# Decode attention in four layers: the last output-projection rows over six DMA engines, a bridge of matmuls, a split wo block and a mended head mapping

## Chip, cores, metric

One core of one Trainium2 chip runs the whole program. The metric is device time in microseconds (us); less is better. Each kernel was run several times; all runs quoted here are of the fast state. The profile is one execution, and its times count from the start of its span.

## The reference

Four layers, A, B, A, B, each a residual step of one token. A and B have their own caches and weights; each has 32 heads of width 192, 8192 cached positions and a model width of 640, in bfloat16.

```python
h = layernorm(x)                               # [1, 640]
q = (h @ wq).reshape(32, 192)                  # wq [640, 6144]
p = softmax(q @ k_cache^T * 192**-0.5)         # k_cache [32, 8192, 192]
o = p @ v_cache                                # v_cache [32, 8192, 192]
x = x + o.reshape(6144) @ wo                   # wo [6144, 640]
```

One K or V head is 3 MB. Of the 256 that the four layers use, 250 are loaded from memory (the page counts the loads), so the program is a stream of loads with arithmetic beside it.

## The kernel before

SyncE issues all loads into a pool of 8 slots. VectorE multiplies K by the query, TensorE sums the products, and TensorE multiplies V by the probabilities. The output projection takes 30 heads in three blocks of 10 (`wo`, 1920 rows on 128 partitions). The last two heads come apart, as `wol`: 384 rows of wo, 480 KB, 3 rows for each of 128 partitions. In the last layer, 3 of the 15 row groups of the third block come as a load of their own, `wob`, after `wol`.

```python
# the load of the last rows: one transfer over 128 partitions
if O_PART[l] == P:
    return SP.op(lambda s: s.dma_start(
        wol_rows(l), w["wo"][r0:r0 + O_LAST * DH].rearrange("(p i) n -> p (i n)", p=P)),
        *free, sem=semOL, inc=16)
...
# order of the last steps of a layer: V of heads 28 to 31, the block wo 2, then wol
part += [("v", l, i) for i in range(H - AHEAD, H)]
part.insert(-O_LAST, ("wc", l, 2))
part.insert(-1 if l == 1 else len(part), ("wo", l, 2))   # in layer 1 before V of head 31
...
# a head's gather is kept in `todo` and done at a later step
elif n[0] == "wo":
    if todo is not None:
        todo(); todo = None
    ...
else:                                                     # wol: does not do what is in todo
    last["TT"] = last["TTn"]
    last["oTl"] = ev_y = project(n, wol_rows(l), oTl[0:O_PART[l]], last["TTn"])
```

Two faults stand in it. In layer 1 the V of head 31 is the last step before `wol`, and `wol` does not do the gather that waits in `todo`, so that layer projects an old output of head 31. In layer 3, where heads are taken in another order, `q_spread` and `gather` use the position of a head where they need its number.

Of the kernel before, what the change touches and what calls it, by code (L numbers as in the profile page):

```python
# [71 lines left out]
def build(nc, A_x, A_k, A_v, A_wq, A_wo, B_x, B_k, B_v, B_wq, B_wo, out):  # L72
# [12 lines left out]
    TS = J * DH  # L85
    QW = H * DH
    Q_PARTS = [[(0, 2), (2, 2), (4, 1)] if l < 2 else [(0, 1), (1, 2), (3, 2)] for l in range(NL)]
    O_PART = [P] * NL
    OI = [O_LAST * DH // n for n in O_PART]
    NB = 3  # L90
    G = 4
    FORWARD = dict(heads=list(range(H)), q0=0, q1=Q_FIRST * DH, wo=[0, HEADS_W, 2 * HEADS_W], wol=H - O_LAST)
    BACKWARD = dict(heads=[H - 2, H - 1] + list(range(H - HEADS_W, H - 2)) + list(range(O_LAST, H - HEADS_W))
# [4 lines left out]
    with ExitStack() as ctx:  # L98
# [12 lines left out]
        wq0 = [sb(f"wq0{i}", [P, DC, Q_FIRST * DH], BF16) for i in range(2)]  # L111
        orow = sb("orow", [1, HEADS_W * DH], BF16)
        oT = sb("oT", [P, NW], BF16)
        oTl = sb("oTl", [P, max(OI)], BF16)
        o_sb = sb("o_sb", [P, 2 * DH], F32)
        q_sb = [sb(f"q_sb{i}", [P, DH], BF16) for i in range(3)]
        qT = sb("qT", [P, H * DH // P], BF16)
# [65 lines left out]
        def head(l, p):  # L183
            return ORDER[l]["heads"][p]
# [12 lines left out]
        for l in range(NL):  # L197
            if l < 2:
                plan.append(("wq", l, 0))
                steps += [("wq", l, g) for g in range(3)]  # L200
            elif l == 2:
                plan += [("wq", l, g) for g in range(3)]
                steps.append(("wq", l, 0))
            else:
                plan.append(("wq", l, 0))
                steps.append(("wq", l, 0))
            for p in range(H):
                if p in (HEADS_W, 2 * HEADS_W):
                    b = p // HEADS_W - 1
                    steps += [("wc", l, b), ("wo", l, b)]  # L210
                    plan.append(("wo", l, b))
                if first_load("k", l, p) == ("k", l, p):
                    plan.append(("k", l, p))
                if stays("k", l, p):
                    plan.append(("t", l, p))
                if l == 2 and p == 0:
                    part = [("m", l, 0), ("wq", l, 1), ("s", l, 0), ("v", l, 0), ("wq", l, 2)]
                elif p < H - AHEAD:
                    part = [("m", l, p), ("s", l, p), ("v", l, p)]
                else:  # L220
                    part = [("m", l, p)]
                    if p > H - AHEAD:
                        part.append(("s", l, p - 1))
                    if p == H - 1:
                        part.append(("s", l, p))
                        part += [("v", l, i) for i in range(H - AHEAD, H)]
                        part.insert(-O_LAST, ("wc", l, 2))
                        part.insert(-1 if l == 1 else len(part), ("wo", l, 2))
                steps += part
                plan += [n for n in part if n[0] == "wo" or n[0] == "v" and first_load(*n) == n]  # L230
                if l == 3 and p == 1:
                    for g in (1, 2):
                        plan.append(("wq", l, g))
                        steps.append(("wq", l, g))
            plan.append(("wol", l))
            steps.append(("wol", l))
        plan.append(("wob", NL - 1))
        at = {n: i for i, n in enumerate(steps)}

        def released(n):  # L240
# [40 lines left out]
                return pool[:, i + c0 * QW:i + (c0 + k) * QW].rearrange("p (c n) -> p c n", c=k)  # L281
            return slot[place[("wq", l, g)]][:, 0:k * QC].rearrange("p (c n) -> p c n", c=k)

        def wol_rows(l):

            if l + 1 == NL:
                i = place[("wol", l)] * TS
            else:
                i = place[("wq", l + 1, 0)] * TS + (DC * QW if l == 0 else QC)
            return pool[0:O_PART[l], i:i + OI[l] * D]  # L290

        def transfer(n):
            l = n[1]
# [2 lines left out]
            free = [freed[b] for b in before[n]]  # L296
            if n[0] == "wol":
                r0 = o["wol"] * DH
                if O_PART[l] == P:
                    return SP.op(lambda s: s.dma_start(  # L300
                        wol_rows(l), w["wo"][r0:r0 + O_LAST * DH].rearrange("(p i) n -> p (i n)", p=P)),
                        *free, sem=semOL, inc=16)
                k = O_PART[l] // O_LAST
                for h in range(O_LAST):
                    e = SP.op(lambda s, h=h: s.dma_start(
                        wol_rows(l)[h * k:(h + 1) * k],
                        w["wo"][r0 + h * DH:r0 + (h + 1) * DH].rearrange("(q e i) n -> e q (i n)", e=8, i=OI[l])),
                        *free, sem=semOL, inc=16)
                return e
            if n[0] == "t":  # L310
# [68 lines left out]
        def layer(l, ev_z, ev_true):  # L379
# [56 lines left out]

            def q_spread(h):

                c0 = h * DH
                PE.wait(last["qT"], last["QB"], ev_const)  # L440
                done = 0
                while done < DH:
                    b, o = divmod(c0 + done, P)
                    n = min(P - o, DH - done)
                    e = PE.op(lambda t, b=b, o=o, n=n, d=done: t.matmul(  # L445
                        QM[:, d:d + n], lhsT=qT[:, b:b + 1].broadcast_to([P, P]), rhs=ident[:, o:o + n],
                        start=True, stop=True), signal=(done + n == DH), bank=use["QM"])
                    done += n
                last["qbc"] = e
                i = (l * H + h) % 3  # L450
                ev_q[h] = last["QB"] = AC.op(
                    lambda a: a.activation(q_sb[i][:], QM[:, 0:DH], ACT.Copy), e, last["q"][i], bank=use["QM"])  # L452
# [2 lines left out]

            def project(n, rows, o, ev_o):

                t3 = rows.rearrange("p (i n) -> p i n", n=D)
                k = t3.shape[1]
                end = n == ("wob", l) or n == ("wol", l) and l + 1 < NL  # L460
                PE.wait(ev_o, need(n), last["YB"])
                for i in range(k):
                    for c in range(DC):
                        e = PE.op(lambda t, i=i, c=c, f=y_first[0], fin=end and i == k - 1: t.matmul(  # L464
                            YB[:, c:c + 1], lhsT=t3[:, i, c:D:DC], rhs=o[:, i:i + 1], start=f, stop=fin,
                            skip_group_check=True), signal=(i == k - 1 and c == DC - 1), bank=use["YB"])
                        y_first[0] = False
                freed[n] = e
                return e

            def columns(k):

# [62 lines left out]
            def values(h):  # L535
# [16 lines left out]
                if h < H - O_LAST:  # L552
                    parts = [(o_sb[:], OB[par][:, 0:2 * DH])]
                else:
                    q = 1 if O_PART[l] == P else O_PART[l] // O_LAST // 8
                    parts = [(o_sb[:, i * DH:(i + 1) * DH].rearrange("p (i e q) -> p q e i", i=OI[l], q=q),
                              OB[par][:, i * DH:(i + 1) * DH].rearrange("p (q e i) -> p q e i", i=OI[l], q=q))
                             for i in range(2)]
                for o, i in parts:
                    ev_os[h] = AC.op(lambda a, o=o, i=i: a.activation(o, i, ACT.Copy, scale=rl[pi][:, 0:1]),  # L560
                                     e, ev_rl[h], last["osb"], bank=use[f"O{par}"])
                last["O"][par] = last["rl"][pi] = ev_os[h]

            def gather(h):

                PE.wait(ev_os[h], last["TO"], ev_const)
                for i in range(2):
                    e = PE.op(lambda t, i=i: t.matmul(TB[0:1, C_O:C_O + DH], lhsT=pick[:, i:i + 1],  # L568
                                                      rhs=o_sb[:, i * DH:(i + 1) * DH], start=(i == 0), stop=(i == 1)),
                              signal=(i == 1), bank=use["TB"])  # L570
                last["osb"] = e
                o0 = (h % HEADS_W) * DH
                last["TO"] = last["row_written"] = AC.op(
                    lambda a: a.activation(orow[0:1, o0:o0 + DH], TB[0:1, C_O:C_O + DH], ACT.Copy), e, last["orow"], bank=use["TB"])  # L574

            def gather_last(h):

                n = O_PART[l] // O_LAST
                k = OI[l]
                r0 = (h - (H - O_LAST)) * n  # L580
                PE.wait(ev_os[h], last["TT"], ev_const)
                for c in range(k):
                    for i in range(2):
# [11 lines left out]
            for i, n in enumerate(here):  # L595
# [20 lines left out]
                elif n[0] == "wo":  # L616
# [1 line left out]
                        todo()  # L618
                        todo = None
                    k = NW - NB if n == ("wo", NL - 1, 2) else NW  # L620
                    last["oT"] = project(n, slot[place[n]][:, 0:k * D], oT[:, 0:k], last["oTw"])
                else:
                    last["TT"] = last["TTn"]
                    last["oTl"] = ev_y = project(n, wol_rows(l), oTl[0:O_PART[l]], last["TTn"])
                    if l + 1 == NL:
                        ev_y = project(("wob", l), slot[place[("wo", l, 2)]][:, (NW - NB) * D:NW * D], oT[:, NW - NB:NW], last["oTw"])
                following = [m[2] for m in here[i + 1:] if m[0] == "m" and m[2] not in ev_q][:1]
                if q_ready and following and n[0] in ("m", "v", "wc", "wo", "wq") and (n[0] == "wq" or following[0] <= n[2] + 2):
                    q_spread(following[0])
# [66 lines left out]
```

## Time and profile before

| | before |
|---|---|
| time, median (3 runs) | 1997.03 us (1996.98 to 1997.15) |
| moved | 849.67 MB, mean 426 GB/s |
| busy: TensorE, VectorE | 70%, 53% of the span |

The first lines are from the profile's page: the span, then the span in 40 equal slices, with DMA busy in tenths and GB/s.

```profile
span 1994.7 us, 20387 instructions
...
DMA  9999999999999999999999999999999999999998
GB/s 411 431 431 428 431 428 430 430 432 429 429 429 431 428 432 429 429 431 428 430 384 431 430 429 432 428 430 429 430 430 426 429 431 429 431 429 430 430 429 344
DMA packets 40487, 849.67 MB, mean 426 GB/s; under 512 B 4688, under 2 KB 4688, under 8 KB 5328
```

The stream runs at about 430 GB/s everywhere but at the start, in the slice of the passage from layer 1 to layer 2 (384) and at the end (344).

The passage between layers 1 and 2, from the timeline (start, duration, engine, line, operation, output<-inputs, shapes, count; in brackets the idle time before and what ended it):

```profile
1010.47 3.16 PE L464 MATMUL YB<-oT,pool 128*128 128x1 bf16 x75
...
1017.58 2.73 PE L545 MATMUL O<-pool,p_sb 128*2 128x384 bf16 x32 [3.96 <-DMA pool<-in_B_v_cache_dram]
...
1020.24 0.77 PE L464 MATMUL YB<-oTl,pool 128*128 128x1 bf16 x15
1020.36 0.95 ACT L560 ACTIVATE o_sb<-O,small 128x192 f32<-128x192 f32 x2 [9.62 <-PE O L545]
...
1034.77 0.34 SPq L321 DMA_DIRECT2D pool<-in_A_k_cache_dram  x1
```

TensorE waits 3.96 us for V of head 31, multiplies it, and projects the last rows at 1020.24, before head 31's output has been evicted (1020.36): the missing gather can be seen. The K load of layer 2 is issued only at 1034.77: by the view of waits, SyncE's queue waits 8.7 us for the score matmuls of layer 2 (L58) that free its slot, and these come after the projection. The groups of instructions show the missing gather by number: 84 matmuls are 7 heads of 12, where four layers have 8 such heads:

```profile
L584 PE MATMUL TB<-small,o_sb 128*64 128x1 f32 x84 | 6.0, 199 | 7.3 <-ACT o_sb L560 7.3
```

The tail of the last layer, from the same view. The last load, `wob`, lands at 1989.98; the last matmul ends 1.5 us later:

```profile
1987.69 2.56 PE L464 MATMUL YB<-oT,pool 128*128 128x1 bf16 x60 [1.17 <-DMA pool<-in_B_wo_dram]
...
1990.11 0.74 PE L464 MATMUL YB<-oTl,pool 128*128 128x1 bf16 x15
...
1990.71 0.74 PE L464 MATMUL YB<-oT,pool 128*128 128x1 bf16 x15
```

One more thing is in the trace, but in no view: the times at which each of the 16 engines reports the landing of its share of a load. They show how far engines have drifted apart. The table was made from these records: the last landing of a load, and how far ahead of it the other engines were.

```
before, last wo block, layer 0: last 510.44, the others ahead by 4.8 4.7 4.6 4.5 4.4 4.4 | 3.1 2.5 | 1.6 ... 1.3 us
before, last wob:               last 1989.98, the others ahead by 8.2 8.2 8.0 8.0 7.4 7.1 | 5.7 4.0 | 2.0 ... 0.5 us
```

Six engines run far ahead. They gain nothing by it, for a wait ends with the last of the 16 reports: for V of head 31 of layer 1 the first comes at 1009.67 us, the last at 1017.53, and TensorE starts on it at 1017.58.

### The profile page before, as it was taken

The numbers are of one execution on the slowest core, as the hardware profiler recorded it, in microseconds if no ns is written. First come the engines' busy times: TensorE is split into PE (matmuls) and PEld (weight loads), VectorE is DVE, ScalarE is ACT, GpSimd is POOL, SyncE is SP. The second block draws the span as 40 slices with busy tenths as digits, with TensorE's granted clock in tenths as the row PEclk, the third lists the DMA queues.
The fourth block names the chain that finished last, engine by engine and source line by source line (L and its number), as shares of the span: only waits on it lengthen the run. The fifth ranks groups of instructions, "written<-read, shape, count | busy, mean of one in ns | idle before, by whom it ended". The sixth has DMA issues, their size and how long they took to land.

```text
span 1994.7 us, 20387 instructions
## 1 busy us (share of the span) xinstructions
PE 1392.3 (70%) x10426; PEld 317.9 (16%) x7482; DVE 1047.4 (53%) x1074; ACT 220.2 (11%) x664; POOL 4.5 (0%) x22
## 2 busy tenths in 40 slices
PE   4766767667567766766767676676776777766776
PEld 1111112111311111211031111111112212111112
DVE  3554554556255455455726545545563466554563
ACT  0111111110011111111011111111101111111111
POOL 0000000000000000000000000000000000000000
PEclk9888887888688788888978888878887878888888
DMA  9999999999999999999999999999999999999998
GB/s 411 431 431 428 431 428 430 430 432 429 429 429 431 428 432 429 429 431 428 430 384 431 430 429 432 428 430 429 430 430 426 429 431 429 431 429 430 430 429 344
DMA packets 40487, 849.67 MB, mean 426 GB/s; under 512 B 4688, under 2 KB 4688, under 8 KB 5328
## 3 DMA queue, kind: packets, MB, share of 16 engines
q1 hardware_dynamic: 40256, 848.38, 99.4%
q8 instruction: 70, 1.15, 0.2%
q14 instruction: 17, 0.14, 0.0%
q10 hardware_dynamic: 144, 0.00, 0.0%
HBM read 848.36 MB, written 0.00 MB: 425 GB/s over the span
## 4 chain that ended last, share of the span: by engine, by line
DMA 69%; PE 17%; DVE 12%; ACT 1%; issue 1%; another core or an unknown queue 0%; DVEq 0%
DMA pool<-in_B_k_cache_dram 32%; DMA pool<-in_A_k_cache_dram 30%; PE S L58 11%; DVE pool L494 10%; DMA pool<-in_B_wo_dram 2%; PE O L545 2%; DMA pool<-in_A_wo_dram 2%; DMA pool<-in_B_v_cache_dram 2%; DMA x_bf<-in_A_x_dram 1%; PE S L507 1%; PE TB L568 1%; PE QT L426 1%; DVE s_sb L515 1%; ACT p_sb L525 1%; PE YB L464 1%
## 5 line engine op out<-in xcount | busy, mean ns | idle before, releaser
L494 DVE TENSOR_TENSOR pool<-pool,q_sb 128x3072 bf16<-128x3072 bf16 x512 | 865.5, 1752 | 406.2 <-DMA pool<-in_A_k_cache_dram 207.6
L58 PE MATMUL S<-pool,ident 128*128 128x512 bf16 x2944 | 796.8, 425 | 35.4 <-DVE pool L494 35.4
L545 PE MATMUL O<-pool,p_sb 128*2 128x384 bf16 x4096 | 346.9, 420 | 4.0 <-DMA pool<-in_B_v_cache_dram 4.0
L507 PE MATMUL S<-pool,ident 128*128 128x512 bf16 x128 | 59.7, 467 | 224.7 <-DVE pool L494 224.7
L515 DVE TENSOR_REDUCE s_sb<-S 128x64 f32<-128x512 f32 x128 | 88.3, 690 | 229.2 <-PE S L58 229.2
L568 PE MATMUL TB<-o_sb,small 128*1 128x192 f32 x480 | 123.6, 390 | 38.2 <-DVE small L533 27.1
L545 PEld LDWEIGHTS O<-pool,p_sb 128*2 128x2 bf16 x4096 | 127.9, 88 | 138.0 <-issue 99.2
L452 ACT ACTIVATE q_sb<-QM 128x192 bf16<-128x192 f32 x120 | 39.6, 330 | 956.5 <-PE QM L445 956.5
L445 PEld LDWEIGHTS QM<-ident,qT 128*128 128x128 bf16 x240 | 23.1, 98 | 739.3 <-issue 723.9
L529 PE MATMUL TB<-small,ones 128*128 128x1 f32 x256 | 50.3, 266 | 109.9 <-ACT p_sb L525 109.9
L519 PE MATMUL QM<-ident,m_bf 128*128 128x128 bf16 x128 | 27.8, 217 | 122.9 <-DVE m_bf L518 121.2
L560 ACT ACTIVATE o_sb<-O,small 128x384 f32<-128x384 f32 (+1 forms) x136 | 77.2, 579 | 238.5 <-PE O L545 238.5
L533 DVE RECIPROCAL small<-TB 128x1 f32<-128x1 f32 x128 | 21.5, 168 | 123.0 <-PE TB L529 123.0
L525 ACT ACTIVATE p_sb<-s_sb,small 128x64 bf16<-128x64 f32 x128 | 44.5, 348 | 269.6 <-DVE small L522 269.6
L522 DVE TENSOR_REDUCE small<-QM 128x1 f32<-128x128 f32 x128 | 37.3, 291 | 62.1 <-PE QM L519 62.1
L574 ACT ACTIVATE orow<-TB 1x192 bf16<-1x192 f32 x120 | 38.3, 319 | 202.2 <-PE TB L568 202.2
L529 PEld LDWEIGHTS TB<-small,ones 128*128 128x128 f32 x256 | 39.5, 194 | 130.4 <-ACT p_sb L525 130.4
L507 PEld LDWEIGHTS S<-pool,ident 128*128 128x128 bf16 x128 | 12.7, 99 | 283.9 <-DVE pool L494 283.6
L519 PEld LDWEIGHTS QM<-ident,m_bf 128*128 128x128 bf16 x128 | 12.3, 96 | 215.6 <-ACT q_sb L452 126.9
L568 PEld LDWEIGHTS TB<-o_sb,small 128*1 128x1 f32 x480 | 33.4, 89 | 81.5 <-DVE small L533 36.0
L464 PE MATMUL YB<-oT,pool 128*128 128x1 bf16 x900 | 38.0, 178 | 5.8 <-DMA pool<-in_A_wo_dram 2.3
L464 PEld LDWEIGHTS YB<-oT,pool 128*128 128x128 bf16 x900 | 37.0, 131 | 6.7 <-ACT oT L478 2.9
(50 smaller groups left out, 213.9 us busy)
## 6 DMA issues: line engine op xcount, KB each, us to landing
pool<-in_B_k_cache_dram SPq DMA_DIRECT2D x64, 3072.0 KB, 35.5
pool<-in_A_k_cache_dram SPq DMA_DIRECT2D x63, 3072.0 KB, 27.6
pool<-in_A_v_cache_dram SPq DMA_DIRECT2D x63, 3072.0 KB, 33.7
pool<-in_B_v_cache_dram SPq DMA_DIRECT2D x60, 3072.0 KB, 36.5
pool<-in_A_wo_dram SPq DMA_DIRECT2D x6, 2400.0 KB, 25.5
pool<-in_B_wo_dram SPq DMA_DIRECT2D x5, 2400.0 KB, 34.0
pool<-in_A_wq_dram SPq DMA_DIRECT2D x1, 7680.0 KB, 20.7
pool<-in_B_wq_dram SPq DMA_DIRECT2D x1, 7680.0 KB, 30.5
```

What stands on the lines that cost most here:

```text
L58: return t.add_instruction(mybir.InstMatmult(name=t.bass.get_next_instruction_name(), engine=mybir.EngineType.PE, ins=[t.lower_ap(rhs), t. ...
L452: lambda a: a.activation(q_sb[i][:], QM[:, 0:DH], ACT.Copy), e, last["q"][i], bank=use["QM"])
L464: e = PE.op(lambda t, i=i, c=c, f=y_first[0], fin=end and i == k - 1: t.matmul(YB[:, c:c + 1], lhsT=t3[:, i, c:D:DC], rhs=o[:, i:i + 1], s ...
L494: e = DV.op(lambda v, d0=d0: v.tensor_tensor(k3[:, :, d0:d0 + QD], kin[:, :, d0:d0 + QD], q_sb[qi][:, d0:d0 + QD].unsqueeze(1).broadcast_t ...
L507: t.matmul(S[:, :], lhsT=ident[:], rhs=k3[:, :, d0:d0 + R], start=True, stop=fin) if d0 == 0 else
L515: ev_s = DV.op(lambda v: v.tensor_reduce(s_sb[par][:], S[:].rearrange("p (j r) -> p j r", r=R), AX.X, ALU.add), ev_S[h], last["s"][par], b ...
L519: e = PE.op(lambda t: t.matmul(QM[:, C_MX:C_MX + P], lhsT=m_bf[par][:, 0:1].broadcast_to([P, P]), rhs=ident[:], start=True, stop=True), ev ...
L525: ev_p[h] = AC.op(lambda a: a.activation(p_sb[pi][:], s_sb[par][:], ACT.Exp, bias=negm[par][:, 0:1], accum_out=l_col[par][:]), ev_n, ev_s, ...
L529: e = PE.op(lambda t: t.matmul(TB[:, C_L + par:C_L + par + 1], lhsT=ones[:, 0:1].broadcast_to([P, P]), rhs=l_col[par][:], start=True, stop ...
L545: e = PE.op(lambda e, g=g, j=j, f=m < G, fin=fin: e.matmul(OB[par][32 * g:32 * g + 2, 0:2 * DH], lhsT=p_sb[pi][:, j:j + 2], rhs=t[:, j * D ...
L560: ev_os[h] = AC.op(lambda a, o=o, i=i: a.activation(o, i, ACT.Copy, scale=rl[pi][:, 0:1]), e, ev_rl[h], last["osb"], bank=use[f"O{par}"])
L568: e = PE.op(lambda t, i=i: t.matmul(TB[0:1, C_O:C_O + DH], lhsT=pick[:, i:i + 1], rhs=o_sb[:, i * DH:(i + 1) * DH], start=(i == 0), stop=( ...
```

## The change

Its intent is to give the last rows to engines that are ahead. The author's assumption was that a load split over 6 engines goes to the six that run ahead and relieves the others; the rows move to 48 + 48 partitions (0 to 47 and 64 to 111), 4 rows each, for that. Beside this the change mends the two faults, puts 8 matmuls of no use ("bridging") into layer 1, meant to keep the TensorE clock up while it waits for V (in the profile of before the granted clock is 0.5 from 1011.65 to 1032.13 us, and the 3.96 us of waiting are in it), and in layer 3 splits the last wo block in 8 + 7 row groups, both ahead of `wol`.

```diff
-    O_PART = [P] * NL
-    OI = [O_LAST * DH // n for n in O_PART]
-    NB = 3
+    LE = 6
+    LP = LE * 8
+    OI = DH // LP
+    NB = 7
+    WARM = 8
...
+            if l + 1 == NL:
+                plan.append(("wob", l))
+                steps.append(("wob", l))
             plan.append(("wol", l))
             steps.append(("wol", l))
-        plan.append(("wob", NL - 1))
...
-            return pool[0:O_PART[l], i:i + OI[l] * D]
+            return pool[64 * h:64 * h + LP, i:i + OI * D]
...
                 for h in range(O_LAST):
                     e = SP.op(lambda s, h=h: s.dma_start(
-                        ...
+                        wol_rows(l, h), w["wo"][r0 + h * DH:r0 + (h + 1) * DH].rearrange("(q e i) n -> e q (i n)", e=LE, i=OI)),
                         *free, sem=semOL, inc=16)
...
-                c0 = h * DH
+                c0 = head(l, h) * DH - ORDER[l]["q1"] + Q_FIRST * DH
...
+            def warm():
+                t3 = slot[place[("v", l, H - 2)]]
+                PE.wait(last["S"][1])
+                for i in range(WARM):
+                    PE.op(... SP_[1][:, :], lhsT=ident[:], rhs=t3[:, i * 512:(i + 1) * 512] ...)
...
-                o0 = (h % HEADS_W) * DH
+                o0 = (head(l, h) - ORDER[l]["wo"][h // HEADS_W]) * DH
...
                 else:
+                    if todo is not None:
+                        todo()
+                        todo = None
                     last["TT"] = last["TTn"]
```

(Cut: the projection over two halves of rows, and the permutation of the last heads' outputs that fits the new place of the rows.)

More of the change, by code (lines that the diff above doesn't have):

```diff
@@ L113, in build @@
         oT = sb("oT", [P, NW], BF16)
-        oTl = sb("oTl", [P, max(OI)], BF16)
+        oTl = sb("oTl", [P, OI], BF16)
         o_sb = sb("o_sb", [P, 2 * DH], F32)
@@ L282, in wq_rows, with wol_rows @@
             return slot[place[("wq", l, g)]][:, 0:k * QC].rearrange("p (c n) -> p c n", c=k)
-        def wol_rows(l):
+        def wol_rows(l, h):
             if l + 1 == NL:
@@ L298, in transfer @@
                 r0 = o["wol"] * DH
-                if O_PART[l] == P:
-                    return SP.op(lambda s: s.dma_start(
-                        wol_rows(l), w["wo"][r0:r0 + O_LAST * DH].rearrange("(p i) n -> p (i n)", p=P)),
-                        *free, sem=semOL, inc=16)
-                k = O_PART[l] // O_LAST
                 for h in range(O_LAST):
                     e = SP.op(lambda s, h=h: s.dma_start(
-                        wol_rows(l)[h * k:(h + 1) * k],
-                        w["wo"][r0 + h * DH:r0 + (h + 1) * DH].rearrange("(q e i) n -> e q (i n)", e=8, i=OI[l])),
+                        wol_rows(l, h), w["wo"][r0 + h * DH:r0 + (h + 1) * DH].rearrange("(q e i) n -> e q (i n)", e=LE, i=OI)),
                         *free, sem=semOL, inc=16)
@@ L456, in project @@
             def project(n, rows, o, ev_o):
-                t3 = rows.rearrange("p (i n) -> p i n", n=D)
-                k = t3.shape[1]
-                end = n == ("wob", l) or n == ("wol", l) and l + 1 < NL
                 PE.wait(ev_o, need(n), last["YB"])
-                for i in range(k):
-                    for c in range(DC):
-                        e = PE.op(lambda t, i=i, c=c, f=y_first[0], fin=end and i == k - 1: t.matmul(
-                            YB[:, c:c + 1], lhsT=t3[:, i, c:D:DC], rhs=o[:, i:i + 1], start=f, stop=fin,
-                            skip_group_check=True), signal=(i == k - 1 and c == DC - 1), bank=use["YB"])
-                        y_first[0] = False
+                for r, (row, oc) in enumerate(zip(rows, o)):
+                    t3 = row.rearrange("p (i n) -> p i n", n=D)
+                    k = t3.shape[1]
+                    for i in range(k):
+                        for c in range(DC):
+                            end = r == len(rows) - 1 and i == k - 1
+                            e = PE.op(lambda t, i=i, c=c, r=r, f=y_first[0], fin=end and n[0] == "wol", t3=t3, oc=oc: t.matmul(
+                                YB[:, c:c + 1], lhsT=t3[:, i, c:D:DC], rhs=oc[:, i:i + 1], start=f, stop=fin,
+                                tile_position=(64 * r, 0), skip_group_check=True), signal=(i == k - 1 and c == DC - 1), bank=use["YB"])
+                            y_first[0] = False
+                    PE.wait(e if r + 1 < len(rows) else None)
                 freed[n] = e
                 return e
+            def warm():
+                t3 = slot[place[("v", l, H - 2)]]
+                PE.wait(last["S"][1])
+                for i in range(WARM):
+                    PE.op(lambda t, i=i: (t.matmul if i == 0 else lambda *a, **k: matmul_held(t, *a, **k))(
+                        SP_[1][:, :], lhsT=ident[:], rhs=t3[:, i * 512:(i + 1) * 512], start=True, stop=True),
+                        signal=(i == WARM - 1), bank=use["S1"])
             def columns(k):
@@ L554, in values @@
                 else:
-                    q = 1 if O_PART[l] == P else O_PART[l] // O_LAST // 8
-                    parts = [(o_sb[:, i * DH:(i + 1) * DH].rearrange("p (i e q) -> p q e i", i=OI[l], q=q),
-                              OB[par][:, i * DH:(i + 1) * DH].rearrange("p (q e i) -> p q e i", i=OI[l], q=q))
+                    parts = [(o_sb[:, i * DH:(i + 1) * DH].rearrange("p (i e q) -> p q e i", i=OI, e=LE),
+                              OB[par][:, i * DH:(i + 1) * DH].rearrange("p (q e i) -> p q e i", i=OI, e=LE))
                              for i in range(2)]
                 for o, i in parts:
-                    ev_os[h] = AC.op(lambda a, o=o, i=i: a.activation(o, i, ACT.Copy, scale=rl[pi][:, 0:1]),
-                                     e, ev_rl[h], last["osb"], bank=use[f"O{par}"])
-                last["O"][par] = last["rl"][pi] = ev_os[h]
+                    ev_os[h] = last["O"][par] = last["rl"][pi] = AC.op(
+                        lambda a, o=o, i=i: a.activation(o, i, ACT.Copy, scale=rl[pi][:, 0:1]),
+                        e, ev_rl[h], last["osb"], bank=use[f"O{par}"])
             def gather(h):
@@ L576, in gather_last @@
             def gather_last(h):
-                n = O_PART[l] // O_LAST
-                k = OI[l]
-                r0 = (h - (H - O_LAST)) * n
+                n = LP
+                k = OI
+                r0 = (h - (H - O_LAST)) * 64
                 PE.wait(ev_os[h], last["TT"], ev_const)
@@ L620, in layer @@
                     k = NW - NB if n == ("wo", NL - 1, 2) else NW
-                    last["oT"] = project(n, slot[place[n]][:, 0:k * D], oT[:, 0:k], last["oTw"])
-                else:
+                    last["oT"] = project(n, [slot[place[n]][:, 0:k * D]], [oT[:, 0:k]], last["oTw"])
+                    if n == ("wo", 1, 2):
+                        warm()
+                elif n[0] == "wob":
+                    project(n, [slot[place[("wo", l, 2)]][:, (NW - NB) * D:NW * D]], [oT[:, NW - NB:NW]], last["oTw"])
+                else:
+                    if todo is not None:
+                        todo()
+                        todo = None
                     last["TT"] = last["TTn"]
-                    last["oTl"] = ev_y = project(n, wol_rows(l), oTl[0:O_PART[l]], last["TTn"])
-                    if l + 1 == NL:
-                        ev_y = project(("wob", l), slot[place[("wo", l, 2)]][:, (NW - NB) * D:NW * D], oT[:, NW - NB:NW], last["oTw"])
+                    last["oTl"] = ev_y = project(n, [wol_rows(l, h) for h in range(O_LAST)],
+                                                         [oTl[64 * h:64 * h + LP] for h in range(O_LAST)], last["TTn"])
                 following = [m[2] for m in here[i + 1:] if m[0] == "m" and m[2] not in ev_q][:1]
```

## The prediction

> **What bounds it.** The page shows 849.67 MB moved at a mean of 426 GB/s, DMA 9 tenths in nearly every slice, PE 70%, DVE 53%: the stream of K and V tiles is the limit. The change moves the same bytes, so only edges can move. The stretch table shows two: the passage from layer 1 to layer 2 (383 GB/s from 1000 to 1050 us) and the tail (DMA share 0.60 from 1982 us, nothing after 1990).
>
> **The engines are uneven.** Every load adds 16 increments to its semaphore, one for each DMA engine. The trace's landing times of one load spread over 1.8 us at 59 us, 7.9 us at 1018, 2.1 us after the passage (1046), 8.25 us at the end. Six engines run ahead; about ten lose 1.5 us each in turn, in step with the 16 KB instruction fetches (70 on q8). The wait always ends with the slowest. The last wo rows (480 KB) cost each engine 30 KB, 1.16 us (1988.82 to 1989.98). [...] If those are the six ahead, all four last-wo loads leave the slow engines: -1.16 us each; the six gain 50 KB, 1.9 us, and stay just ahead. That the lowest are the fast ones, the trace doesn't show.
>
> **Added work.** Last-wo projection: 40 matmuls of 48 rows for 15, at the measured 41 ns: +1.05 us and a wait between the halves, in each layer. The group table shows the gather of the last heads 84 times, 7 heads of 12: the kernel before never gathers head 31 of layer 1. The change does, on the passage's chain: by the same steps in layer 3 (eviction 0.95, gather 0.86, copy 0.17, gaps) +2.3 us. Against that stand 8 bridging matmuls in PE's idle time of 3.96 us (timeline, 1013.6 to 1017.6). Before, the granted clock was 0.5 from 1011.65 to 1032.13 us; at full clock values take 1.47 for 2.73 us, and score matmuls end about 1.5 us sooner.
>
> **Sum.**
> - Layer 0: -1.16 us at the slow engines.
> - Passage: the chain from V 31's landing to the next K load's issue (1017.5 to 1034.8 us) gets +2.3 +1.2 -1 to -4 us; the engines are realigned there, so it swallows the gain of layers 0 and 1. Net about 0, +-1.
> - Layers 2 and 3: -2.3 us.
> - Tail: before, the big wo part landed at 1987.65 and 90 matmuls followed to 1991.45, 1.5 us after the last byte. Now wob (1120 KB) lands last on the slow engines and 35 + 40 matmuls follow: 3.1 us and a wait of 0.2. +1.8 us.
>
> In all -0.5 to -1 us: **1996.2 us, 8 in 10 between 1994.0 and 1998.2**. Faster by over 2% 0.005, within 2% 0.99, slower 0.005.
>
> **What would show it.** End spread down from 8.25 to about 2-4 us; last-wo matmuls 160 for 60, gather on 8 heads; PE from the last wob landing to the end about 3.2 us; the clock back at 1.0 before 1025 us; next K load's issue within 1 us of 1034.8.
>
> **What would make it wrong.** The lowest engines are slow ones (+3 us); the bridge fails and the passage grows by 2-3 us; the bridge works better than its chain costs (-2 us); an instruction fetch hits the slowest engine once more or less (+-1.5 us).

Which engines a load over fewer than 16 goes to, no trace shows. "The lowest" in the forecast, and in an expectation below, are the engines that the author took such a load to go to; the traces do not number engines. About 0 for layers 0 and 1 and the passage, -2.3 for layers 2 and 3 and +1.8 for the tail come to -0.5 us, of which the forecast made -0.5 to -1. The -1.16 us for each layer were the author's estimate.

## More of the kernel before

The next is the view of stretches, at the end of layer 0 where `wol` comes. A row has the stretch, its length, the busy time of each engine (with its instructions), the granted TensorE clock, the DMA share and GB/s. Share and rate count each packet whole in the stretch in which it starts, so that a stretch can show a share over 1.

```profile
core 0: us, PE busy (x) PEld busy (x) DVE busy (x) ACT busy (x) POOL busy (x), PEclk, DMA share, GB/s
505.00:515.00 10.00, 6.15 (x135) 5.24 (x128) 0.43 (x5) 1.22 (x4) 0.00 (x0) 0.74 1.08 459
515.00:525.00 10.00, 0.36 (x2) 0.27 (x2) 0.80 (x5) 0.00 (x0) 0.55 (x1) 0.50 0.96 415
```

The load of the last rows is not to be seen in it: 459 GB/s is as good as any stretch.

## The result and the profile after

The changed kernel takes 2015.67 us (median of 4 runs, 2014.91 to 2016.85) beside 1997.01 us for the kernel before, which has 4 runs by now. The ratio is 1.0094, with an interval from 1.0077 to 1.0112. Ratios are the mean time of one kernel's fast runs over that of the other's of the same rounds, so not quite the ratio of the medians. The change is within 2%, as forecast, but 18.7 us slower and far outside the stated range.

The page:

```profile
span 2015.1 us, 20689 instructions
...
DMA  9999999999999999999989999999999999999996
GB/s 410 430 429 430 431 430 428 431 429 429 398 431 429 429 429 430 430 430 430 429 333 429 432 429 431 429 429 429 431 430 398 431 427 430 430 429 430 431 429 285
DMA packets 40344, 849.69 MB, mean 422 GB/s; under 512 B 4672, under 2 KB 4672, under 8 KB 5056
```

The same bytes come at 422 instead of 426 GB/s, and the loss is in four places, at the end of each layer: 398 where it was 429, 333 for 384, 398 for 426 and 285 for 344. DMA counts as busy all the same. The stretches at the end of layer 0:

```profile
505.00:515.00 10.00, 5.98 (x135) 5.08 (x135) 0.00 (x0) 1.95 (x6) 0.00 (x0) 0.86 1.14 328
515.00:525.00 10.00, 2.81 (x51) 2.50 (x49) 1.23 (x10) 0.00 (x0) 0.55 (x1) 0.50 0.96 408
```

A DMA share of 1.14 at 328 GB/s, where it was 1.08 at 459: engines hold packets for longer and move less. A packet of `wol` (5120 bytes now) takes 196 ns at the very end, when no other load is left (the last 16 packets of layer 3), and 350 ns in the mean of layer 0. The packets of before (3840 bytes) took 149 ns (median) with all 16 engines at it. Both undisturbed figures come to 26 GB/s for one engine.

The passage:

```profile
1018.34 3.16 PE L463 MATMUL YB<-oT,pool 128*128 128x1 bf16 x75
...
1021.36 0.59 PE L476 MATMUL S<-pool,ident 128*128 128x512 bf16 x1
...
1021.75 2.89 PE L58 MATMUL S<-pool,ident 128*128 128x512 bf16 x7
1024.56 1.47 PE L554 MATMUL O<-pool,p_sb 128*2 128x384 bf16 x32
...
1029.74 1.95 PE L463 MATMUL YB<-oTl,pool 48*128 48x1 bf16 x40 [1.76 <-DMA pool<-in_B_wo_dram]
...
1044.67 0.34 SPq L319 DMA_DIRECT2D pool<-in_A_k_cache_dram  x1
```

Behind the bridge (1021.36 and 1021.75) the clock is up: the granted clock is 1.0 from 1024.19 to 1031.01 us, and values take 1.47 us instead of 2.73. But after the gather of head 31, TensorE still waits 1.76 us for the last rows, and the K load goes out 10 us later than before. In the tail the last rows, which the prediction had landing ahead of `wob`, come 3 us after it:

```profile
2006.54 1.56 PE L463 MATMUL YB<-oT,pool 128*128 128x1 bf16 x35 [0.64 <-DMA pool<-in_B_wo_dram]
...
2009.72 1.94 PE L463 MATMUL YB<-oTl,pool 48*128 48x1 bf16 x40 [1.62 <-DMA pool<-in_B_wo_dram]
```

The group of the gather now counts 128, 8 heads of 16 (4 row groups instead of 3), where it was 84:

```profile
L592 PE MATMUL TB<-small,o_sb 128*48 128x1 f32 x128 | 7.0, 184 | 8.6 <-ACT o_sb L569 8.6
```

The shift between the two profiled runs, from the landing of the same loads: +1.7 us when the last wo block of layer 0 has landed, +4.8 at the next load (wq), +9.7 at the first K of layer 2, +16.2 at the first wo part of the last block. Before the first `wol` it was +0.4. So in each of layers 0 to 2 `wol` costs some 4 to 6 us (in layer 1 the new gather is in it), and the loss stays.

### The profile page after: what moved, and what is told of

It reads as the page before. It is cut to its first block, busy times and chain, and to the rows that moved or that the text cites. A ratio compares the mean times of both kernels' runs of the same rounds, so it can differ in the third digit from the quotient of the medians.

```text
span 2015.1 us, 20689 instructions
## 1 busy us (share of the span) xinstructions
PE 1397.8 (69%) x10578; PEld 321.8 (16%) x7627; DVE 1047.7 (52%) x1074; ACT 220.9 (11%) x665; POOL 4.5 (0%) x22
## 3 DMA queue, kind: packets, MB, share of 16 engines
q8 instruction: 71, 1.16, 0.2%
## 4 chain that ended last, share of the span: by engine, by line
DMA 69%; PE 18%; DVE 12%; ACT 1%; issue 1%; SPq 0%; another core or an unknown queue 0%; DVEq 0%
DMA pool<-in_B_k_cache_dram 32%; DMA pool<-in_A_k_cache_dram 30%; PE S L58 12%; DVE pool L503 10%; DMA pool<-in_B_wo_dram 4%; PE O L554 2%; DMA pool<-in_A_wo_dram 2%; DMA x_bf<-in_A_x_dram 1%; PE TB L576 1%; PE S L516 1%; PE QT L424 1%; DVE s_sb L524 1%; ACT p_sb L534 1%; PE TB L538 1%; PE YB L463 1%
## 5 line engine op out<-in xcount | busy, mean ns | idle before, releaser
L554 PE MATMUL O<-pool,p_sb 128*2 128x384 bf16 x4096 | 338.3, 412 | 0.0
```

The lines of the kernel that those rows point to most:

```text
L554: e = PE.op(lambda e, g=g, j=j, f=m < G, fin=fin: e.matmul(OB[par][32 * g:32 * g + 2, 0:2 * DH], lhsT=p_sb[pi][:, j:j + 2], rhs=t[:, j * D ...
```

## Theories and experiments

- **Port theory.** The supposition that engines slow each other by where in SBUF they write: split over six engines, the rows go to partitions 0 to 47 and 64 to 111, and there they would meet what other engines write at the same time. Which engine writes which partitions, and through what, no trace or run here shows. It is tested below by other partitions and another split. "Own" partitions, in an expectation and in the names of two runs, are those that the author took each engine to write in the large loads.
- **Source theory.** The guess that six engines which read neighbouring blocks of 5 KB in memory slow each other there.
- **Third theory.** The six engines that get the load are not the ones ahead, so that 50 KB more for each (80 KB instead of 30) lengthen the slowest ones.
- **Chain theory.** The time is lost in the longer chain between layers 1 and 2, by the gather or the bridge.

Times below stand beside runs of the kernel before on the same chip. A difference to it is one of medians. Within one session the kernel before ranged from 1995.78 to 1999.23 us, so a difference of 1 us says little.

| run | time, us | before, us | difference | packets of wol, mean ns in layers 0 to 3 |
|---|---|---|---|---|
| the change | 2015.67 | 1997.01 | +18.7 | 350, 298, 333, 240 |
| all_engines | 1999.99 | 1996.51 | +3.5 | 155, 150, 151, 154 (3840 B) |
| own_port | 2002.95 | 1996.51 | +6.4 | 198, 197, 198, 196 |
| k16_96 | 2010.04 | 1996.51 | +13.5 | 336, 277, 357, 244 |
| mend_only | 1998.77 | 1996.51 | +2.3 | 151, 150, 150, 150 (3840 B) |
| no_bridge | 2000.09 | 1996.53 | +3.6 | not read |
| other_port | 2023.10 | 1996.53 | +26.6 | 386, 364, 379, 285 |
| split | 1996.46 | 1996.53 | -0.1 | not read |
| split_reorder | 1995.40 | 1995.98 | -0.6 | not read |
| mend_again | 2000.04 | 1995.98 | +4.1 | not read |

The results of all experiments were correct in the comparison. The packet times come from the trace's DMA packet records, all packets of that size.

### all_engines: the load back on 128 partitions

```diff
-    LE = 6
-    LP = LE * 8
+    LE = 1
+    LP = 64
...
-                for h in range(O_LAST): ... "(q e i) n -> e q (i n)" ...
+                return SP.op(lambda s: s.dma_start(
+                    wol_rows(l), w["wo"][r0:r0 + O_LAST * DH].rearrange("(p i) n -> p (i n)", p=P)),
+                    *free, sem=semOL, inc=16)
```

> The changed kernel, but its last wo rows come as before the change: one load of 480 KB to 128 partitions, 3 rows each, over all 16 DMA engines. Mended mapping, the gather of head 31 in layer 1, bridging matmuls and the order of the wo parts stay. If the load on 6 engines is the whole cause (both port theory and source theory), the 18.7 us go: 1995 to 1999 us, 3840-byte packets back at 150 ns. If the cost comes from the longer chain between layers 1 and 2 (gather, bridge) or from the tail, it stays over 2008 us.

1999.99 us (1999.54 to 2000.91), 1 us over the stated range. The stretch at the end of layer 0 is as before the change:

```profile
505.00:515.00 10.00, 7.47 (x148) 6.39 (x148) 1.14 (x10) 1.29 (x5) 0.00 (x0) 0.87 1.08 459
```

The way in which the last rows are loaded costs 15.2 of the 18.7 us (18.7 - 3.5). The chain theory can explain at most the other 3.5.

### own_port: six engines, partitions 0 to 23 and 32 to 55

Each load is cut in two, of 24 partitions each: both heads' rows now go to partitions 0 to 23 and 32 to 55, side by side. The blocks read in memory, the size of packets and the number of engines stay. The expectation below says that the order of reads stays too; it does not quite: in the order of the code, six neighbouring blocks still come at a time, but every second group of six comes first, in a load of its own. Partitions 24 to 31 are multiplied by zeros.

```diff
+                    for g in range(2):
                         e = SP.op(lambda s, h=h, g=g: s.dma_start(
-                            wol_rows(l, h), ....rearrange("(q e i) n -> e q (i n)", e=LE, i=OI)),
+                            wol_rows(l)[32 * g:32 * g + 24, h * OI * D:(h + 1) * OI * D],
+                            ....rearrange("(a g e i) n -> g e a (i n)", g=2, e=LE, i=OI)[g]),
```

> The changed kernel, still 6 engines, packets of 5120 bytes and the same order of reads in memory[...]. Port theory[...]: packets fall from a mean of 350, 298, 333 ns in layers 0 to 2 to under 215 ns, and the time to 1993 to 1999 us. Source theory (six engines read neighbouring 5 KB blocks of memory and slow each other there): packets stay near 300 ns or more and the time over 2010 us. Third theory (the six lowest engines are simply not the ones ahead, so their 50 KB more come on top): packets near 200 ns, yet 2001 to 2008 us.

Packets fall to 196 to 198 ns, and 12.2 of the 18.7 us go (18.7 - 6.4, before rounding). The source theory falls: six neighbouring blocks of 5 KB still come at a time in the order of the code, and for that it forecast 300 ns or more. The stretch has nearly its rate back:

```profile
505.00:515.00 10.00, 6.94 (x201) 6.30 (x202) 0.00 (x0) 2.19 (x8) 0.00 (x0) 0.73 1.03 439
```

But 2002.95 us is 3.0 us more than with all engines, where it should have been less. The landing records say why. The engines' lead on the slowest one, at the last wo block of layer 0, ahead of `wol`, and at the first load after it (wq):

```
own_port, wo:    4.1 4.0 3.9 3.8 3.5 3.4 | 2.6 1.7 0.9 0.8 0.7 0.6 0.6 0.4 0.0 0.0 us
own_port, wq:    6.1 6.0 5.8 | 3.4 3.3 3.3 3.3 2.9 2.5 2.5 2.2 2.0 1.7 1.5 0.1 0.0 us
```

Three of the six leaders keep their lead on the unloaded engines: they carried nothing. The landings of `wol` itself say it directly. Each of its six engines reports four times, 0.8 us apart, and the first reports come 0.8 us after the shares of the wo block whose leads were 4.0, 3.9, 3.5, 2.6, 1.7 and 0.6 us. So of the six engines that carry `wol` three are among the six leaders and three are not, and the latter fall behind. That is the third theory. It is worth at most these 3.0 us: own_port also has 40 matmuls for 15 in each last projection (1.76 us for 0.76 in the passage), and no run parts the two. In the tail of the two profiles, the last `wol` lands 2.9 us later (1995.86 and 1992.97). Which three numbers they are, no run shows.

### k16_96: sixteen engines on the same 96 partitions

```diff
-   .rearrange("(q e i) n -> e q (i n)", e=LE, i=OI)
+   .rearrange("(q i) n -> q (i n)", i=OI)
```

> The changed kernel with the last rows on the same 96 partitions, 4 rows each, in two loads as now, but split over 16 engines (3 partitions each). Port theory: [...]packets of 5120 bytes take well over 250 ns in the mean, but each engine carries only 30 KB: 1 to 2 us more per layer than on 128 partitions, 1998 to 2004 us. Source theory and third theory: packets near 196 ns and the time within 1.5 us of the run with 128 partitions.

2010.04 us (2009.01 to 2010.62), more than I had expected of either theory. Packets take 336, 277 and 357 ns in layers 0 to 2, although the load is split over 16 engines (each half lands in 16 shares), 30 KB for each if the shares are equal. Partitions are those of the change again, 0 to 47 and 64 to 111.

```profile
505.00:515.00 10.00, 5.00 (x86) 3.81 (x79) 0.00 (x0) 1.10 (x3) 0.00 (x0) 0.50 1.07 310
```

This rules out that six engines as such were the trouble. The port theory had the direction right, but 1 to 2 us for each layer was too small: the loads beside and behind are held up too (310 GB/s in this stretch, 459 with all_engines).

### other_port: six engines, partitions 64 to 87 and 96 to 119

Like own_port, but everything 64 partitions higher.

```diff
-                            wol_rows(l)[32 * g:32 * g + 24, ...],
+                            wol_rows(l)[64 + 32 * g:64 + 32 * g + 24, ...],
```

> The run with six engines on their own partitions, moved up by 64 partitions[...]. Port theory: [...]packets of 5120 bytes slow down, mean over 240 ns in layers 0 to 2, and the time is 4 to 12 us over the run on own partitions, 2006 to 2015 us. If only sharing within the load matters (or runs of 8 partitions, or two loads instead of four): packets at 197 ns and 2002 to 2004 us.

2023.10 us (2022.60 to 2024.48), 20 us more than own_port for one number, and worse than the port theory's own range. Packets take 386, 364 and 379 ns in layers 0 to 2, with a median of 401 in layer 0: twice 196. Split and packets are those of own_port; what the packets meet here, they meet from other loads, for without these they take 196 ns (below).

```profile
505.00:515.00 10.00, 3.12 (x113) 2.63 (x114) 0.00 (x0) 1.62 (x6) 0.00 (x0) 0.79 1.08 251
```

251 GB/s at a DMA share of 1.08, for 439 at 1.03 in own_port, is the clearest sign of it. One rival is left by the design: partitions 64 and up could simply be slow for these six engines. The packet records exclude it. The last 16 packets of layer 3, after all other loads have ended, take 196 ns in the mean (204 at most) at the very same partitions. And the engines slow each other: around the `wol` of layer 0, 33 of the 88 packets of the wo block (19200 bytes) take over 1300 ns, where in before and in own_port none takes over 730. With own_port this pair settles that the partitions decide: same split, same source, same packets, only the partitions differ (and, with them, the rows of TensorE that multiply them). That much of the port theory is shown; that a port stands behind it is not.

### mend_only and mend_again: the two mends alone

```diff
-                c0 = h * DH
+                c0 = head(l, h) * DH - ORDER[l]["q1"] + Q_FIRST * DH
...
-                o0 = (h % HEADS_W) * DH
+                o0 = (head(l, h) - ORDER[l]["wo"][h // HEADS_W]) * DH
...
                 else:
+                    if todo is not None:
+                        todo()
+                        todo = None
```

> The kernel before with the two mends alone (head mapping of layer 3; gather of head 31 in layer 1), no other part of the change. Prediction's reading: the gather lengthens the chain between layers 1 and 2 by 2.3 us, of which the passage swallows none or up to half: 1997.5 to 2000 us. If the passage has slack, 1997 us. If the mapping or the gather cost what the change lost, over 2010 us.

> The kernel before with the two mends alone once more, beside the others on the same chip: 1998 to 2000 us, so 1.5 to 3 us over the kernel before and 2 to 4 us over the reordered one. If the first result was noise of the runs: within 1 us of the kernel before.

1998.77 us (1998.38 to 2001.23), and in the second session 2000.04 us (1998.44 to 2000.64): 2.3 and 4.1 us over before. The first ratio (1.0007, interval 0.9991 to 1.0024) did not tell it from nothing; the second (1.0015, 1.0001 to 1.0029) just does. So the mends cost 2 to 4 us by the medians (1.4 and 3.0 by the ratios), about as much as all_engines has over before (3.5). The passage, from the profile of mend_only, which is its slowest run (2001.23 us):

```profile
1014.98 3.16 PE L464 MATMUL YB<-oT,pool 128*128 128x1 bf16 x75
...
1018.07 2.69 PE L545 MATMUL O<-pool,p_sb 128*2 128x384 bf16 x32
...
1020.81 0.94 ACT L560 ACTIVATE o_sb<-O,small 128x192 f32<-128x192 f32 x2 [5.55 <-PE O L545]
...
1021.80 0.86 PE L584 MATMUL TB<-small,o_sb 128*64 128x1 f32 x12 [1.04 <-ACT o_sb L560]
...
1022.92 0.76 PE L464 MATMUL YB<-oTl,pool 128*128 128x1 bf16 x15 [0.26 <-ACT oTl L589]
...
1037.54 0.34 SPq L321 DMA_DIRECT2D pool<-in_A_k_cache_dram  x1
```

From the end of values (1020.76) to the projection (1022.92) pass 2.2 us where before it was nothing; the K load goes out at 1037.54 instead of 1034.77. TensorE did not wait for V at all here. The wo projection ended 4.5 us later than in the profile of before. About 1 us of this was there at 985 us already; the rest came with a granted clock of 0.81 in the mean from 985 to 1012 us instead of 0.99 (values at 1002.05 took 2.73 us, where those at 999.97 had taken 1.47).

### no_bridge: all engines, no bridging matmuls

```diff
-    WARM = 8
+    WARM = 0
...
-                    if n == ("wo", 1, 2):
+                    if WARM and n == ("wo", 1, 2):
                         warm()
```

> The run with all 16 engines again, without the 8 bridging matmuls. If the bridge works as the prediction had it (PE at full clock through the passage), leaving it out costs 1 to 3 us: 2001 to 2003 us. If, as the traces of that run and of the mend alone suggest (values start 2.8 us later behind the bridge and run 1.2 us shorter), it buys nothing: within 1 us of the run with it, near 1999 to 2000.5 us.

2000.09 us (1998.24 to 2001.89) beside 1999.99 with the bridge, in another session; over the kernel before of its own session each has 3.6 and 3.5 us. The bridge buys nothing that can be measured. In the trace of all_engines, V had landed by the time the bridge was at work, so values stood behind it:

```profile
1014.46 3.16 PE L461 MATMUL YB<-oT,pool 128*128 128x1 bf16 x75
...
1017.78 3.19 PE L58 MATMUL S<-pool,ident 128*128 128x512 bf16 x7 [0.16 <-issue]
1020.90 1.50 PE L552 MATMUL O<-pool,p_sb 128*2 128x384 bf16 x32
```

Values start 2.8 us later than in mend_only (1018.07) and are 1.2 us shorter (1.50 for 2.69).

### split and split_reorder: a shorter chain in the passage

In split, layer 1 does what the change does in layer 3 alone: V 31 comes ahead of the last wo block, and the block comes in parts of 8 and 7. After the last landing only 15 matmuls are left. In split_reorder the first part is also projected before the gather of head 31, while TensorE would wait for that head's eviction. Both have the mends, all 16 engines, and no bridge. In the cut below, the lines on `todo` are split_reorder's alone.

```diff
+    SPLIT = (1, NL - 1)
-                        part.insert(-1 if l == 1 else len(part), ("wo", l, 2))
+                        part.append(("wo", l, 2))
-            if l + 1 == NL:
+            if l in SPLIT:
                 plan.append(("wob", l))
                 steps.append(("wob", l))
...
                 elif n[0] == "wo":                       # split_reorder
-                    if todo is not None:
+                    if todo is not None and not (n[2] == 2 and l in SPLIT):
...
                 elif n[0] == "wob":
+                    if todo is not None:
+                        todo()
+                        todo = None
```

> All 16 engines, no bridge, and in layer 1 what the change does in layer 3 alone: V 31 comes before the last big wo block, which comes in parts of 8 and 7 rows, so that after the last landing only 15 matmuls stay before the layer norm instead of values, eviction, gather, copy and 15 matmuls. If the passage between layers 1 and 2 is bound by this chain, as the rows from V 31's landing to the next K load's issue say, it shortens by 2.5 to 3.5 us and the time falls to 1996 to 1998.5 us. If the passage is bound by something else (slots, clock), it stays within 1 us of the run without a bridge.

> The run with the split wo block in layers 1 and 3, with one more step: the first part of the block is projected before the gather of head 31, in the time in which PE waits for the eviction of that head. In that run's trace PE was busy from the gather at 1987.5 us to the last matmul at 1992.0, two us past the last landing (1990.0). If the tail is bound by this row of matmuls, 0.5 to 1 us go there and up to 1 us in the passage: 1995 to 1996.3 us, not over the kernel before. If landings bind, no change: 1996.5 us.

1996.46 us (1995.08 to 1997.55) for split: 3.6 us less than no_bridge in the same session. 1995.40 us (1994.60 to 1996.11) for split_reorder, beside 1995.98 for before: a ratio of 0.9995, interval 0.9983 to 1.0008. That is the same time as before, with the right heads, and some 20 us less than the change. What the reorder adds to the split (-0.6 for -0.1 us against before, in two sessions) is inside the scatter. The passage of split_reorder:

```profile
1014.51 1.47 PE L556 MATMUL O<-pool,p_sb 128*2 128x384 bf16 x32
1015.91 1.76 PE L462 MATMUL YB<-oT,pool 128*128 128x1 bf16 x40
1016.03 0.99 ACT L571 ACTIVATE o_sb<-O,small 128x192 f32<-128x192 f32 x2 [1.25 <-PE O L556]
1017.61 0.86 PE L594 MATMUL TB<-small,o_sb 128*64 128x1 f32 x12
1018.40 1.56 PE L462 MATMUL YB<-oT,pool 128*128 128x1 bf16 x35
1019.82 0.74 PE L462 MATMUL YB<-oTl,pool 128*128 128x1 bf16 x15
...
1034.15 0.34 SPq L318 DMA_DIRECT2D pool<-in_A_k_cache_dram  x1
```

Matmuls fill the time of the eviction, the last rows are projected at 1019.82, and the K load goes out at 1034.15, 3.4 us ahead of mend_only. (In the profiles of split and no_bridge, which differ in the split alone, it goes out at 1034.24 and 1036.44.) The passage was bound by this chain, not by the slots alone.

## Why the prediction was wrong, point by point

- **What bounds the kernel: right.** The time followed the DMA rate. "The change moves the same bytes, so only edges can move" was right about the place: the loss is in the four slices at layer ends. It was silent on the possibility that the same bytes come at a lower rate.
- **"-1.16 us each; the six gain 50 KB, 1.9 us": the step that failed.** The 1.9 us took for granted that an engine keeps its 26 GB/s wherever it writes. Instead, on partitions 0 to 47 and 64 to 111, packets took 350 ns in the mean of layer 0 for 196, and the loads beside them slowed down too (328 GB/s in the stretch for 459): where 1.16 us less were forecast for a layer, layers 0 to 2 each took 4 to 6 us more. With the rows on partitions 0 to 23 and 32 to 55, 12.2 us came back.
- **"If those are the six ahead ... the trace doesn't show": failed, and had been named as a risk of +3 us.** Three of six are ahead. With the rows on those partitions, six engines still cost 3.0 us more than all sixteen, the longer projection included.
- **"End spread down from 8.25 to about 2-4 us": wrong.** It was 13.5 us at the first wo part of the last block. The slowest engine fell further behind.
- **Gather of head 31, +2.3 us: right in size** (2.2 us in the trace of the mend), and the group table shows it (8 heads of 16, as 4 row groups need). **"The passage swallows the gain, net about 0": wrong.** The mends alone cost 2.3 and 4.1 us in two sessions. The chain binds, as the gain by the split shows.
- **Bridge: half right.** Values ran at a granted clock of 1.0, 1.47 for 2.73 us. But the idle time of 3.96 us that it was to fill belonged to one profile; in the profile of the mend it was not there. No net gain was measured.
- **Tail, +1.8 us: wrong order.** The prediction had `wol` landed before `wob`; it landed 3.1 us after it (2009.59 and 2006.49), and 40 matmuls came after that. With all engines the split tail is no longer than before: in no_bridge the last matmul ends 1.0 us after the last landing (1992.88 and 1991.83), before the change it was 1.5 us (1991.45 and 1989.98).
- **Last-wo matmuls: 160 as predicted**, at 49 ns each (1.95 us for 40) where 41 ns had been taken.

The 18.7 us are thus 12.2 for the choice of partitions, 3.0 for six engines in place of sixteen (with the longer projection), and 3.5 for the rest, which the mends alone match (2.3 and 4.1). The last is not split further: bridge and tail are below the scatter of the runs. Left open is also why engines fall behind in step with the 16 KB instruction fetches, and which engines are spared. In the profile of before one engine's lag grows from 1.6 to 3.2 us between the loads that land at 255.10 and 263.63, with a fetch at 255.3; from 21 to 503 us the lags of all engines behind the first grow by 27.5 us together, over 16 fetches (70 in the whole span, of 1.06 us in the mean). The correlation was read from the trace and not tested.

## What to carry to other kernels

Before a load is put on fewer or other partitions, try the places and read its packets: the same rows, split over six engines alike, took 198 ns a packet in layer 0 on partitions 0 to 23 and 32 to 55, and 386 ns on 64 to 87 and 96 to 119, with 20 us between the two programs. A busy DMA share at a lower rate in the stretches (1.14 at 328 GB/s for 1.08 at 459) was the sign here that engines stood in each other's way. A load that is given to engines that are ahead helps only if it is known which ones they are, and the landings of each engine before and after one such load tell it (own_port, with three of its six ahead, was 3.0 us over all_engines). Where a stream of loads has to be restarted between two layers, shorten what lies between the last landing and the next issue: splitting the last weight block and using the time of an eviction gave back all that the correction had cost (1995.40 us beside 1995.98 for before). And a bridge that fits one profile need not fit the next: in the unchanged part before the passage, 985 to 1012 us in, the granted clock was 0.99 in one profile and 0.81 in another, and a projection ended 4.5 us later.
